# A retention and MLP kernel: eight load requests for the first weight matrix are renumbered

## The chip, the cores and the metric

The kernel runs on one core of a Trainium2 chip. The metric is the device time of one execution in microseconds. A core has five engines that run side by side, each through its own instructions in order: PE (matrix products, with its weight loads listed as PEld), DVE (elementwise work), ACT (activation functions and copies), POOL (elementwise work, and the requests for some transfers) and SP (the requests for the other transfers). They wait for each other by semaphores. Transfers between the main memory and the core's own memory are done by 16 DMA engines that all the requests share.

## The reference

For 8 batches, 8 heads, 576 positions and a head size of 64, a retention layer is computed: scores of q and k, times a decay that falls with the distance and is zero ahead of the position, times v. Its result x, one row of 512 numbers for each of the 4608 tokens, goes through a two-layer MLP with a tanh GELU between.

```python
scores = scale * np.matmul(q, k.transpose(0, 1, 3, 2))
Dmat = np.where(rel >= 0, gamma[:, None, None] ** rel[None, :, :], 0.0)
ret = scores * Dmat[None, :, :, :]
attn_out = np.matmul(ret, v)
x = attn_out.transpose(0, 2, 1, 3).reshape(B * S, H * D)      # 4608 x 512
h = x @ w_in                                                  # 512 x 2048
g = 0.5 * h * (1.0 + np.tanh(c * (h + 0.044715 * h * h * h)))
out = g @ w_out                                               # 2048 x 512
```

## The kernel before, in words

**Tiling.** A batch is cut into five units of positions: four of 128 and a tail of 64. The units are numbered through, so 40 in all. The MLP works on nine blocks of 512 tokens. Matrix products take fp16 and add up in fp32 in PSUM banks.

**The order is written out by hand.** `ORDER` (lines 17 to 123) is a list of steps, and the loop at line 1044 issues them one after the other. Each engine gets its instructions in the order of this list. A step is a letter with numbers, and `do` (line 1030) tells which function it calls. The steps that matter here:

| step | function, line | what it does |
|---|---|---|
| `I,g,g` | `load_w_in`, 248, through `load_w`, 236 | POOL requests piece g of w_in, cast to fp16 on the way (line 238) |
| `J,g,g` | `load_w_out`, 258 | POOL requests piece g of w_out |
| `L,u,n` | `load`, 208 | SP requests q, k or v of unit u |
| `N,t,fc,part` | `mm1`, 750 | PE: 256 hidden columns (fc and fc+1, of 128 each) for half a token block: 8 matrix products at line 757 |
| `F,t,fc,part` | `gelu`, 764 | ACT: GELU of what `N` computed |
| `Y`, `X`, `R` | 624, 609, 653 | PE: scores, state products and output of a pair of wide units (lines 636, 619, 665 and 677) |
| `t`, `y` | `pe_T`, 489, `copy_T`, 498 | PE transposes (line 493), and the copy of what they gave |
| `a`, `m`, `z` | 703, 684, 724 | sums of the state (DVE, line 713), masking (DVE, line 644), cast of the state (POOL) |
| `K,n` | `busy`, 999 | n matrix products on an identity that nobody reads (line 1003) |
| `O,t,u` | `mm2`, 777 | PE: a quarter of the second layer's sum for 128 tokens, line 783 |

**The pieces of w_in.** w_in is 512 x 2048. Piece g is a block of 256 rows and 512 columns, by `f, c = divmod(g, 2)`: f is the block of columns (hidden blocks 4f to 4f+3) and c is the half of the rows. So pieces 0 and 1 are the two halves of f=0, 2 and 3 of f=1, 4 and 5 of f=2, 6 and 7 of f=3. All eight are of one size, 256 KB as they land.

**How mm1 reads them.** One `N` step computes its two blocks of 128 hidden columns one after the other, and each is four products over the four quarters of the 512 rows: quarters 0 and 1 lie in the even piece, 2 and 3 in the odd piece. So the first two of its 8 products need the even piece alone, and the third needs the odd one.

```python
for i in range(TB // n):
    for ct in range(NCT):
        nc.tensor.matmul(
            hps[:, i, :],
            w_in_sb[:, ct, 128 * (fc + i) : 128 * (fc + i) + 128],
```

**The order of PE's steps around the change** (lines 21 to 23 of the list, PE's steps alone): `R,0`, `Y,2,1`, `K,3`, `N,0,2,0`, `N,0,0,0`, `N,0,12,0`, `Y,2,0`, `N,0,4,0`, `X,2`, `t,4,k`, `t,4,q`, `N,0,8,0`, `N,0,10,0`, `R,2`. By the hidden columns, these first readers are of f=0 (`N,0,2` and `N,0,0`), f=3 (`N,0,12`), f=1 (`N,0,4`) and f=2 (`N,0,8`), in that order.

**The order on POOL.** The eight `I` steps stand at eight places among POOL's other work: the first behind the setup, the second behind the decay rows, then three in a row, a cast of k, and three in a row again. In this document the places are called s1 to s8.

Of the kernel before, what the change touches and what calls it, by code (L numbers as in the profile page):

```python
# [14 lines left out]
I32 = mybir.dt.int32  # L15

ORDER = """
L,0,1 b Z,1,v L,0,0 L,0,2 L,2,1 L,2,0 I,2,g q,0 k,0,g Z,2,g g,g I,7,g K,4 K,4 K,4 K,3 K,4 t,0,q,h
L,2,2 L,4,1 c t,0,k,h I,1,g v,0,v X,0 y,0,k,v I,0,g I,3,g a,0,1 y,0,q,v Z,3,v k,2,g K,4 K,4 Y,0,1
t,2,k,o m,0,1 z,0,1,a I,6,g K,4 Y,0,0 a,1,1 q,2 L,4,0 K,4 t,2,q,h m,0,0 y,2,k,a y,2,q,v I,4,g K,1  # L20
R,0 I,5,g x,0 Y,2,1 L,5,0 x,1 i,4,v K,3 N,0,2,0 N,0,0,0 o,1,1 m,2,1 L,5,1 Z,4,g v,2,v F,0,2,0
N,0,12,0 Y,2,0 F,0,0,0 z,1,1,v N,0,4,0 L,5,2 X,2 k,4,g Z,5,v q,4 F,0,12,0 F,0,4,0 t,4,k,o a,2,1
t,4,q,o a,3,1 y,4,q,a N,0,8,0 L,4,2 z,2,1,g L,9,1 N,0,10,0 F,0,8,0 k,5,g m,2,0 L,7,1 R,2 F,0,10,0
y,4,k,v B,4,-1 q,5 x,3 x,2 N,0,14,0 L,7,0 t,5,q,o N,0,0,1 L,7,2 J,1,g F,0,14,0 N,0,6,0 y,5,q,v J,3,g
# [1051 lines left out]
```

## Time and profile before

| what | value |
|---|---|
| time, median of 3 runs (lowest to highest) | 297.25 us (296.75 to 297.45) |
| time of the profiled execution | 296.55 us |
| its span in the profile | 294.8 us |
| PE busy | 281.6 us, 96% of the span |
| DVE, ACT, POOL busy | 73%, 51%, 38% |
| transfers | 36.70 MB read, 9.44 MB written |
| requests for w_in | 8 on POOL, median 9.1 us from request to landing |

The profile has one line for each group of like instructions: its line of code, engine, operation, the tile that it writes `<-` the tiles that it reads, count, time busy and mean, and the idle time of the engine ahead of it with what ended that. The timeline lists instructions in order of time: start, duration, engine, line, tiles, count, and in brackets the idle time before. The chain that ended last goes back from the last instruction through whatever released each step. A busy PE is not a PE at its peak, since matrix products overlap: a product of 128x256 is listed with 273 ns, but in a row they start about 109 ns apart.

### The profile page before, as it was taken

The page shows a single profiled execution, that of the slowest core. Times are in us where ns is not written, and L with a number is a line of the kernel's source. Part 1 is how long each engine was busy: PE and PEld are TensorE (multiplying, and loading weights), DVE is VectorE, ACT ScalarE, POOL GpSimd, SP SyncE. Part 2 cuts the span into 40 slices and gives each one's busy share as a digit, 9 for nine tenths or more (in the row PEclk, how much of TensorE's full clock was granted, in tenths as well). Part 3 has the DMA queues.
Part 4 walks back from the last instruction along what each step waited for, and adds up shares of the span by engine and source line. Part 5 has one row for each costly group of instructions (what it writes and reads, how often), then busy time and mean ns, then how long its engine had stood idle before and what let it go on. Part 6 is the DMA issues. An engine that isn't in the chain of part 4 may idle for free.

```text
span 294.8 us, 9645 instructions
## 1 busy us (share of the span) xinstructions
PE 281.6 (96%) x4067; PEld 235.7 (80%) x4067; DVE 214.7 (73%) x437; ACT 149.9 (51%) x288; POOL 111.8 (38%) x178
## 2 busy tenths in 40 slices
PE   7686999999999999999999999999999999999995
PEld 2354986667888888888888888888888888888873
DVE  7694763686865779576678699599889988977740
ACT  2143674334634553554554646546777587665411
POOL 7941920404361084163415644783466223000000
PEclk9999999999999999999999999999999999999999
DMA  6999999995989999999099997899488570002112
GB/s 192 284 252 242 221 219 211 217 205 129 244 119 247 167 190 213 207 248 216 17 239 197 183 196 169 202 189 161 130 194 197 75 216 6 37 26 83 73 42 103
DMA packets 136428, 49.79 MB, mean 169 GB/s; under 512 B 118208, under 2 KB 130880, under 8 KB 136384
## 3 DMA queue, kind: packets, MB, share of 16 engines
q1 hardware_dynamic: 132032, 44.97, 75.5%
q0 software_dynamic: 4352, 4.20, 8.6%
q8 instruction: 32, 0.52, 0.8%
q14 instruction: 12, 0.10, 0.1%
HBM read 36.70 MB, written 9.44 MB: 156 GB/s over the span
## 4 chain that ended last, share of the span: by engine, by line
PE 84%; DMA 6%; POOL 5%; DVE 2%; issue 1%; ACT 1%; ACTq 0%; POOLq 0%
PE bank L860 30%; PE bank L757 27%; PE bank L957 12%; PE bank L783 6%; DMA w_in_sb<-in_moe_w_in_dram 4%; PE x L529 2%; PE sk L553 2%; DMA pages<-in_k_dram 2%; POOL w_in_sb L238 1%; PE sk L563 1%; PE x L574 1%; DVE pages L817 1%; POOL wide L269 1%; DMA out_dram<-ost 1%; PE bank L493 1%
## 5 line engine op out<-in xcount | busy, mean ns | idle before, releaser
L757 PE MATMUL bank<-xT,w_in_sb 128*128 128x256 f16 x768 | 94.4, 273 | 2.9 <-DMA w_in_sb<-in_moe_w_in_dram 2.9
L765 ACT ACTIVATE gT<-bank 128x512 f16<-128x512 f32 x96 | 56.7, 598 | 62.4 <-PE bank L757 60.5
L757 PEld LDWEIGHTS <-w_in_sb 128*128 128x128 f16 x768 | 73.7, 98 | 14.5 <-DMA w_in_sb<-in_moe_w_in_dram 3.7
L860 PEld LDWEIGHTS <-ssum 128*128 128x128 f16 x480 | 46.3, 98 | 6.4 <-issue 0.8
L269 POOL CAST sz<-s 64x256 f16<-64x256 f32 x48 | 24.5, 510 | 66.1 <-DVE s L713 44.8
L860 PE MATMUL bank<-tsum,ssum 128*128 128x256 f16 x360 | 46.0, 273 | 0.6 <-DVE ost L817 0.6
L860 PEld LDWEIGHTS <-gT 128*128 128x128 f16 x360 | 34.7, 98 | 4.4 <-issue 0.2
L424 POOL TENSOR_TENSOR qk<-pages,dec 128x512 f16<-128x512 f32 (+1 forms) x20 | 21.5, 1087 | 32.5 <-PE x L619 12.5
L860 PE MATMUL bank<-w_out_sb,gT 128*128 128x256 f16 x240 | 31.1, 273 | 0.0
L424 POOL TENSOR_TENSOR v<-pages,dec 128x512 f16<-128x512 f32 (+1 forms) x20 | 21.5, 1074 | 14.2 <-DMA pages<-in_v_dram 11.4
L817 DVE TENSOR_TENSOR ssum<-gT 128x1024 f16<-128x1024 f16 x30 | 23.5, 784 | 4.1 <-ACT gT L765 3.7
L817 DVE TENSOR_TENSOR ost<-u,bank 128x256 f32<-128x256 f32 x45 | 18.1, 415 | 9.4 <-PE bank L860 9.1
L817 DVE TENSOR_TENSOR ssum<-gT,ssum 128x1024 f16<-128x1024 f16 x30 | 23.4, 781 | 0.2
L691 DVE TENSOR_TENSOR ret<-sk,mask 128x512 f16<-128x512 f32 (+1 forms) x32 | 19.8, 617 | 4.7 <-PE sk L563 4.4
L957 PEld LDWEIGHTS <-pages 128*128 128x128 f16 x192 | 18.4, 98 | 2.8 <-issue 0.3
L957 PE MATMUL bank<-pages 128*128 128x256 f16 x144 | 20.3, 273 | 0.3 <-ACT pages L267 0.3
L783 PE MATMUL bank<-w_out_sb,gT 128*128 128x512 f16 x80 | 19.1, 380 | 0.0
L817 DVE TENSOR_TENSOR u<-u,bank 128x256 f32<-128x256 f32 x30 | 12.4, 415 | 8.8 <-PE bank L860 5.9
L593 ACT ACTIVATE xT<-x 128x512 f16<-128x512 f32 (+1 forms) x25 | 14.3, 578 | 7.9 <-PE x L574 7.9
L713 DVE TENSOR_TENSOR s<-s,sk 128x256 f32<-128x256 f32 x36 | 14.9, 414 | 4.6 <-PE sk L563 4.0
L817 DVE TENSOR_TENSOR hc<-hc,bank 128x512 f32<-128x512 f32 x21 | 14.4, 684 | 4.8 <-PE bank L957 2.3
L267 ACT COPY hc<-bank 128x512 f32<-128x512 f32 x19 | 11.1, 585 | 12.5 <-PE bank L957 12.5
(114 smaller groups left out, 428.3 us busy)
## 6 DMA issues: line engine op xcount, KB each, us to landing
out_dram<-ost SPq DMA_DIRECT2D x35, 256.0 KB, 3.4
pages<-in_q_dram SPq DMA_DIRECT2D x32, 256.0 KB, 4.7
pages<-in_v_dram SPq DMA_DIRECT2D x24, 256.0 KB, 4.0
pages<-in_k_dram SPq DMA_DIRECT2D x24, 256.0 KB, 4.3
pages<-in_k_dram SPq DMA_DIRECT2D x4, 512.0 KB, 7.0
pages<-in_v_dram SPq DMA_DIRECT2D x4, 512.0 KB, 6.6
w_in_sb<-in_moe_w_in_dram POOLq DMA_DIRECT2D x8, 256.0 KB, 9.1
w_out_sb<-in_moe_w_out_dram POOLq DMA_DIRECT2D x8, 256.0 KB, 10.5
```

Of the source, the lines that this page charges most:

```text
L267: nc.scalar.copy(out=o, in_=i)
L269: (nc.vector if eng == "v" else nc.gpsimd).tensor_copy(out=o, in_=i)
L424: eng.tensor_tensor(out=out, in0=s["raw"][:, i, 0:n], in1=dec[:, i // 2, s["j"], 0:n].unsqueeze(2).to_broadcast([128, n, D]), op=ALU.mult,)
L593: nc.scalar.activation(out=xT[:, :, o : o + G * (b - a)].rearrange("c p (h s) -> c p h s", s=G), in_=x[:, a:b].rearrange("c h p s -> c p h ...
L691: nc.vector.tensor_tensor(out=ret[:, :, 0:n], in0=now["two"][:, :, 0, 0:n], in1=mask.unsqueeze(1).unsqueeze(1).to_broadcast([128, 2, n, G] ...
L713: nc.vector.tensor_tensor(out=s32, in0=state[0], in1=kv, op=ALU.add)
L757: nc.tensor.matmul(hps[:, i, :], w_in_sb[:, ct, 128 * (fc + i) : 128 * (fc + i) + 128], xT[:, ct, TB * t % XR + lo : TB * t % XR + hi], st ...
L765: nc.scalar.activation(out=gTs[t][:, fc : fc + TB // (hi - lo), lo:hi], in_=h.pop((t, fc, lo)), func=AF.Gelu_apprx_tanh, bias=0.0, scale=1.0,)
L783: nc.tensor.matmul(ops[t, tcc], gTs[t][:, ft, 128 * tcc : 128 * tcc + 128], w_out_sb[:, ft, :], start=(ft == 0), stop=(ft == NFC - 1),)
L817: (nc.vector if eng == "v" else nc.gpsimd).tensor_tensor(out=out, in0=a, in1=b, op=op)
L860: nc.tensor.matmul(p["ps", bank][:, HN * col : HN * col + HN], a[:, k], b[:, k], start=(k == 0 and i in (1, 6)), stop=(k == HK - 1), skip_ ...
L957: nc.tensor.matmul(p["ps", bank][:, n], w[:, c, 128 * n : 128 * n + 128], x[:, c], start=(n == 0 and c == 0 and i in (1, 2, 5)), stop=(c = ...
```

## The change

The eight requests keep their places in the list. What changes is which piece is asked for at which place:

| place | s1 | s2 | s3 | s4 | s5 | s6 | s7 | s8 |
|---|---|---|---|---|---|---|---|---|
| piece before | 2 | 7 | 1 | 0 | 3 | 6 | 4 | 5 |
| piece after | 1 | 0 | 6 | 2 | 4 | 5 | 7 | 3 |

```diff
-L,0,1 b Z,1,v L,0,0 L,0,2 L,2,1 L,2,0 I,2,g q,0 k,0,g Z,2,g g,g I,7,g K,4 K,4 K,4 K,3 K,4 t,0,q,h
-L,2,2 L,4,1 c t,0,k,h I,1,g v,0,v X,0 y,0,k,v I,0,g I,3,g a,0,1 y,0,q,v Z,3,v k,2,g K,4 K,4 Y,0,1
-t,2,k,o m,0,1 z,0,1,a I,6,g K,4 Y,0,0 a,1,1 q,2 L,4,0 K,4 t,2,q,h m,0,0 y,2,k,a y,2,q,v I,4,g K,1
-R,0 I,5,g x,0 Y,2,1 L,5,0 x,1 i,4,v K,3 N,0,2,0 N,0,0,0 o,1,1 m,2,1 L,5,1 Z,4,g v,2,v F,0,2,0
+L,0,1 b Z,1,v L,0,0 L,0,2 L,2,1 L,2,0 I,1,g q,0 k,0,g Z,2,g g,g I,0,g K,4 K,4 K,4 K,3 K,4 t,0,q,h
+L,2,2 L,4,1 c t,0,k,h I,6,g v,0,v X,0 y,0,k,v I,2,g I,4,g a,0,1 y,0,q,v Z,3,v k,2,g K,4 K,4 Y,0,1
+t,2,k,o m,0,1 z,0,1,a I,5,g K,4 Y,0,0 a,1,1 q,2 L,4,0 K,4 t,2,q,h m,0,0 y,2,k,a y,2,q,v I,7,g K,1
+R,0 I,3,g x,0 Y,2,1 L,5,0 x,1 i,4,v K,3 N,0,2,0 N,0,0,0 o,1,1 m,2,1 L,5,1 Z,4,g v,2,v F,0,2,0
```

## The prediction

> **What bounds the kernel now.** I read the page first. Its chain that ended last lies mostly on PE, with a share for DMA:
>
> ```profile
> PE 84%; DMA 6%; POOL 5%; DVE 2%; issue 1%; ACT 1%; ACTq 0%; POOLq 0%
> ```
>
> Next I asked for the busy time by stretch. Columns: stretch, its length, then PE, PEld, DVE, ACT and POOL busy with their counts, PE's granted clock, DMA share, GB/s.
>
> ```profile
> 20.00:30.00 10.00, 7.00 (x113) 5.01 (x113) 5.68 (x11) 4.82 (x8) 1.35 (x4) 1.00 1.15 243
> 30.00:40.00 10.00, 10.00 (x184) 8.87 (x182) 7.68 (x12) 6.77 (x12) 8.56 (x13) 1.00 1.07 221
> 40.00:50.00 10.00, 10.00 (x152) 7.72 (x150) 4.74 (x5) 6.46 (x11) 0.00 (x0) 1.00 1.22 216
> ```
>
> PE has holes before 30 us and none behind. The change lies in the first stretch. The chain in order of time (start, length, what) tells which wait ends last there:
>
> ```profile
> 15.33 1.38 POOL w_in_sb L238 x2
> 16.71 12.46 DMA w_in_sb<-in_moe_w_in_dram
> 29.17 0.05 issue
> 29.21 1.70 PE bank L757 x14
> 30.92 0.45 PE x L665 x8
> ```
>
> It is the eighth request for w_in: asked for at 16.71, landed at 29.17, and from there PE never stops. So the time hangs on how much PE work is left when the last piece lands. PE's timeline shows it step by step:
>
> ```profile
> 20.46 0.82 PE L1003 MATMUL bank<-ident 128*128 128x512 f16 x3
> 21.12 1.91 PE L757 MATMUL bank<-xT,w_in_sb 128*128 128x256 f16 x16
> 25.35 1.05 PE L757 MATMUL bank<-xT,w_in_sb 128*128 128x256 f16 x8 [2.31 <-DMA w_in_sb<-in_moe_w_in_dram]
> 26.32 0.42 PE L636 MATMUL sk<-qkT 64*64 64x128 f16 x16
> 26.67 1.05 PE L757 MATMUL bank<-xT,w_in_sb 128*128 128x256 f16 x8
> 27.65 0.45 PE L619 MATMUL x<-wide,wide 64*64 64x64 f16 x32
> 28.03 0.40 PE L493 MATMUL bank<-ident,qk 128*128 128x128 f16 x4
> 28.26 0.38 PE L757 MATMUL bank<-xT,w_in_sb 128*128 128x256 f16 x2
> 29.21 1.70 PE L757 MATMUL bank<-xT,w_in_sb 128*128 128x256 f16 x14 [0.57 <-DMA w_in_sb<-in_moe_w_in_dram]
> 30.75 0.44 PE L665 MATMUL x<-qkT,sz 128*128 128x128 f16 x5
> ```
>
> By lines and counts these are K,3; N,0,2 and N,0,0; N,0,12; Y,2,0; N,0,4; X,2; t,4; two products of N,0,8; its other six with N,0,10; R,2. N,0,8 ran its two products on piece 4 and stopped at the third, which needs piece 5: so the wait is for the half that a product reads, not for the whole group. The table has each place's landing: the request's start in POOL's timeline plus its time to landing, asked for one by one.
>
> | | s1 | s2 | s3 | s4 | s5 | s6 | s7 | s8 |
> |---|---|---|---|---|---|---|---|---|
> | asked | 4.01 | 8.27 | 12.10 | 12.82 | 13.53 | 15.28 | 16.00 | 16.71 |
> | to landing | 8.2 | 7.4 | 7.6 | 8.2 | 10.0 | 10.0 | 11.2 | 12.5 |
> | landed | 12.2 | 15.7 | 19.7 | 21.0 | 23.5 | 25.3 | 27.2 | 29.2 |
>
> The answers for s6, s7 and s8:
>
> ```profile
> DMA to landing us min/median/max: 10.0/10.0/10.0
> ...
> DMA to landing us min/median/max: 11.2/11.2/11.2
> ...
> DMA to landing us min/median/max: 12.5/12.5/12.5
> ```
>
> The 25.35 wait ends with s6 (25.3) and the 29.21 wait with s8 (29.2), so these landings are what PE sees.
>
> **The change part by part.** Nothing is added or removed. The requests keep their places on POOL, and nothing on POOL or SP up to 17 us waits for w_in, so I leave the eight landings where they are and move only the readers.
>
> *Pieces 1 and 0 go from s3, s4 to s1, s2* (landed 15.7 instead of 21.0). N,0,2 gains nothing that counts: K,3's three products of some 0.21 us from 20.46 hold PE to 21.1 anyway, it started at 21.12, and a hole of over 2 us follows. Cost: 0.
>
> *Piece 6 goes to s3 and piece 7 from s2 to s7.* N,0,12 reads both. Its first two products can go at 22.9, when N,0,0 is done; the third waits for 27.2. Six are left: eight products ahead of a step of small ones took 26.67 to 27.65 = 0.98, two of them at 0.109 (1.75 for 16 in the chain) are 0.22, so six are 0.76. N,0,12 ends at 28.0 instead of 26.3, Y,2,0 (26.32 to 26.67, 0.35) at 28.35.
>
> *Piece 3 goes from s5 to s8, 4 and 5 from s7, s8 to s5, s6, and 2 from s1 to s4.* The first unready reader behind Y,2,0 is now N,0,4: two products on piece 2 end at 28.6, the third waits for piece 3 at 29.2. This wait takes the place of N,0,8's. Behind 29.21 PE then has six of N,0,4 (0.76), X,2 (27.65 to 28.03, 0.38), t,4 (0.23), N,0,8 and N,0,10 (16 at 0.109, 1.75): 3.12 us, so R,2 starts at 32.33. Before it was 30.75, so **+1.58 us**. The delay at N,0,12 costs nothing of its own, as 28.6 is 0.6 ahead of 29.2; without that cover each microsecond would cost one.
>
> *Who is queued behind.* X,2 is 2.32 later (29.97 against 27.65), more than R,2 is. On DVE the state sums of line 713 move from 28.16 to 30.5 and the mask of line 644 from 29.02 to 31.3, ending at 32.6. R,2's second part, which reads it, began 0.54 behind its first (31.29), so now at 32.87: 0.3 to spare. The copy for B,4 and the scaling of q for t,5 (30.36, 1.33 long) end at 34.0; t,5 moves from 32.81 to 34.4: fits. POOL waited 8.52 us for the first state sum and cast from 28.64; that and the eight w_out requests behind it (30.55 to 37.85) come 2.3 later. Asked singly, the third, fourth, sixth and eighth of them landed after 9.5, 10.7, 11.3 and 13.3 us, at 41.5, 43.4, 46.9 and 50.4. The first reader of w_out is at 44.91, those of the second to fourth quarters at 47.52, 51.69 and 54.30, and all of them move by 1.6: at least 2.6 are left. Landings could differ among the SP loads that they now meet; by bounds, 0 to about 1 us of it reaching PE. I take 0, nearest to those gaps. ACT has 0.98 of idle in one piece at 38 and follows PE.
>
> *Whether it reaches the end.* PE is full from 29.2, so a delay is handed on unless a later wait eats it. All that PE's waits behind 31 us offer is this:
>
> ```profile
> PE bank L860 <- DVE ost L817: 0.6, 1, 0.6
> PE bank L957 <- DVE pages L817: 0.4, 1, 0.4
> PE bank L957 <- ACT pages L267: 0.3, 1, 0.3
> ```
>
> None ends in a transfer. They lie at 220 to 230 us, and the chain enters them from PE (219.95), so DVE's and ACT's work there shifts along. Bounds: 0 to 1.3 eaten; I take 0.
>
> *Sum.* The profiled execution took 296.55 (span 294.8 and 1.75 around it): 296.55 + 1.58 = 298.13. That execution lies 0.70 below the median of the runs, 297.25, and the result is a median, so I put the same step on it: **298.8 us**, +0.5%. Telling this kernel from no change takes about 0.2%, 0.6 us: its three runs spread over 0.70.
>
> *The longer hole in PE.* Before, the longest was 2.31 us, and the products behind it ran at full pace. Now only two products lie between 23.3 and 27.2, a hole of 3.9 us, which this trace doesn't have. What it has is PE's start: the 19 products of 128x512 from 1.96 on begin 0.43 apart up to 6.63 and 0.21 apart behind it, though the granted clock stands at 1.00 in every stretch. So PE can run at half pace after idleness. Bounds: 0 (as after 2.31 us) to a slow stretch of 4.7 us like the one at the start. I take 0: 3.9 is nearer to 2.31 than to a PE that had never worked. [...]
>
> **The rivals.**
>
> *PE drops to half pace in the hole.* Place: 23.3 to 27.2; it decides if the hole is long enough. Slow for 4.7 us from 27.25: six products 1.4, Y,2,0 0.7, two products 0.45 (29.8, s8 is in), six 1.4, X,2 0.7, which is 31.9; t,4 and 16 products 1.98 at full pace: R,2 at 33.9, 3.15 later than before: 300.4. For: the slow start. Against: full pace after 2.31 us.
>
> *The delay is eaten.* If all 1.3 of PE's later waits go, 297.5. Against: the chain runs through PE into them.
>
> *Faster: the late places land sooner.* s7 and s8 took 11.2 and 12.5, while s2 took 7.4 for the same bytes. Landing after L, R,2 would start at 16.04 + L + 0.76 + 0.35 + 0.98 + 0.38 + 0.23 + 1.75 = 20.5 + L, as s7 then binds. It decides below L = 9.6; at 9.0 R,2 starts at 29.5, and the time is 296.0. For: equal pieces differ by 5 us. Against: the DMA share is at 1.12 to 1.23 throughout 12 to 29 us, and neither sizes, places nor the SP loads change.
>
> *It doesn't do what it says.* The order of first readers is f=0, f=3, f=1, f=2, and in that order the requests would be 1, 0, 6, 7, 2, 3, 4, 5. Piece 7 stands seventh and 3 last. With the literal order N,0,8 would again wait for s8 with the same 14 products behind: 297.25, no change. The diff is what runs, so this is no case of its own, but the reason for the sign.
>
> **How the numbers follow.** N,0,4 waiting for the last piece: 0.73, alone 298.2 to 299.4 (landing of s8 against s7, half a microsecond, and the runs' spread). Half pace: 0.12, 299.8 to 300.6. Eaten: 0.10, 297.2 to 297.8. Faster: 0.05. The first case holds the likeliest time, 298.8. The range from 297.9 to 300.3 leaves out eaten, faster and some of half pace, 0.2 in all. Slower by over 0.2%: the first two, 0.85, less a little for the spread and more for the top of the third: 0.85. Within: 0.10. Faster: 0.05.
>
> **What would show it.** In PE's timeline: N,0,2 still near 21.1; two products of line 757 near 22.9, a wait for w_in ending near 27.2, six products and Y,2,0; two products, a short wait ending near 29.2; then six products, X,2, t,4 and 16 products without a hole, and R,2's line 665 near 32.3. Half pace would show as products of 128x256 starting 0.21 apart behind 27.2. The w_out requests start near 32.9, and no wait for w_out appears at line 783. Wrong would be: another place binding, s7 or s8 landing over 1 us off, a new PE wait for DVE at R,2 or t,5, or waits at 220 to 230 us that shrink by the delay.

## The result, and the profile after

The changed kernel takes 299.57 us (median of 9 runs, 298.48 to 301.04), beside it the kernel before 297.45 (9 runs, 296.75 to 298.76). The ratio is 1.0072, with a 95% interval of 1.0046 to 1.0098: slower by 2.1 us, inside the range, and 0.8 us above the predicted 298.8. The profiled execution took 298.48 us with a span of 296.7. Later the same kernel was timed twice more, each time beside the kernel before: 1.0129 (1.0106 to 1.0153) and 1.0089 (1.0057 to 1.0121).

The page's chain by engine has hardly moved:

```profile
PE 85%; DMA 5%; POOL 4%; DVE 2%; issue 1%; ACT 0%; ACTq 0%; POOLq 0%
```

The chain in order of time (start, length, what) shows another request than before:

```profile
15.33 11.01 DMA w_in_sb<-in_moe_w_in_dram
...
26.38 1.46 PE bank L757 x6
27.84 0.57 PE sk L636 x16
28.41 1.47 PE bank L757 x8
```

It is the seventh request, piece 7, that PE waits for last; behind it PE runs without a stop. PE's timeline of the same stretch:

```profile
21.62 2.13 PE L757 MATMUL bank<-xT,w_in_sb 128*128 128x256 f16 x18
26.38 1.46 PE L757 MATMUL bank<-xT,w_in_sb 128*128 128x256 f16 x6 [2.63 <-DMA w_in_sb<-in_moe_w_in_dram]
27.77 0.64 PE L636 MATMUL sk<-qkT 64*64 64x128 f16 x16
28.35 1.53 PE L757 MATMUL bank<-xT,w_in_sb 128*128 128x256 f16 x8
29.81 0.44 PE L619 MATMUL x<-wide,wide 64*64 64x64 f16 x32
...
30.42 1.91 PE L757 MATMUL bank<-xT,w_in_sb 128*128 128x256 f16 x16
32.17 0.61 PE L665 MATMUL x<-qkT,sz 128*128 128x128 f16 x8
```

The first line holds 18 products: N,0,2, N,0,0 and the first two of N,0,12, as foreseen. Then the hole, the other six, Y,2,0, N,0,4, X,2, t,4, N,0,8 with N,0,10, and R,2 at 32.17, 1.42 us later than before. But six products took 1.39 us from start to the next step's start, and Y,2,0 took 0.58 instead of 0.35. The busy times by stretch say why; the first figure behind the five engines' is PE's granted clock:

```profile
24.00:26.00 2.00, 0.00 (x0) 0.00 (x0) 0.70 (x2) 0.17 (x1) 0.00 (x0) 0.99 1.19 219
26.00:28.00 2.00, 1.62 (x18) 0.96 (x22) 0.00 (x0) 0.12 (x1) 0.00 (x0) 0.50 1.16 261
28.00:29.00 1.00, 1.00 (x20) 0.65 (x13) 0.00 (x0) 0.48 (x1) 0.00 (x0) 0.50 1.13 327
29.00:30.00 1.00, 1.00 (x29) 0.66 (x31) 0.00 (x0) 0.08 (x1) 0.00 (x0) 0.81 0.93 188
```

The clock is at 0.50 from about 25.96 (0.99 over two microseconds is 0.04 us at half) to 29.38 (0.81 over one is 0.38). So the rival "PE drops to half pace in the hole" is there, together with the forecast order of work. In this one execution two things soften it. POOL was 0.67 us ahead of the profile of before, 0.56 of it since a select at line 397 took 0.85 instead of 1.41 us for its pair. Piece 7 landed at 26.3 and piece 3 at 28.3, both 0.9 us ahead of the forecast. And PE, at half pace, came to N,0,4's third product only after piece 3 had landed: the forecast second wait is gone, its place taken by slow work. So it is luck that R,2 came within 0.2 us of the forecast 32.33: from a landing at 28.3 the forecast 3.12 us of work would have brought it to 31.4, and half pace took back most of what the early landing gave.

To follow the delay to the end I compared the starts of 24 marks of PE (the products of line 553) with those of the profile of before. It is 1.42 us at the first, at 69.58 us in the profile before, 1.51 at 191.33 and 1.80 at 241.25. Nothing ate it.

### The profile page after: what moved, and what is told of

Same layout as the page of the kernel before. It is cut to its first block, busy times and chain, and to the rows that moved or that the text cites. A ratio compares the mean times of both kernels' runs of the same rounds, so it can differ in the third digit from the quotient of the medians.

```text
span 296.7 us, 9645 instructions
## 1 busy us (share of the span) xinstructions
PE 284.0 (96%) x4067; PEld 236.6 (80%) x4067; DVE 214.7 (72%) x437; ACT 149.9 (51%) x288; POOL 113.6 (38%) x178
## 4 chain that ended last, share of the span: by engine, by line
PE 85%; DMA 5%; POOL 4%; DVE 2%; issue 1%; ACT 0%; ACTq 0%; POOLq 0%
PE bank L860 30%; PE bank L757 28%; PE bank L957 12%; PE bank L783 6%; DMA w_in_sb<-in_moe_w_in_dram 4%; PE x L529 2%; PE sk L553 2%; DMA pages<-in_k_dram 1%; PE sk L563 1%; PE x L574 1%; PE bank L987 1%; POOL w_in_sb L238 1%; DVE pages L817 1%; PE bank L493 1%; POOL wide L269 1%
## 5 line engine op out<-in xcount | busy, mean ns | idle before, releaser
L757 PE MATMUL bank<-xT,w_in_sb 128*128 128x256 f16 x768 | 95.4, 275 | 2.6 <-DMA w_in_sb<-in_moe_w_in_dram 2.6
L269 POOL CAST sz<-s 64x256 f16<-64x256 f32 x48 | 26.2, 545 | 66.7 <-DVE s L713 46.2
L424 POOL TENSOR_TENSOR qk<-pages,dec 128x512 f16<-128x512 f32 (+1 forms) x20 | 20.8, 1047 | 29.9 <-DMA pages<-in_q_dram 12.0
L424 POOL TENSOR_TENSOR v<-pages,dec 128x512 f16<-128x512 f32 (+1 forms) x20 | 22.2, 1112 | 15.4 <-DMA pages<-in_v_dram 10.9
L817 DVE TENSOR_TENSOR ssum<-gT 128x1024 f16<-128x1024 f16 x30 | 22.9, 764 | 3.5 <-ACT gT L765 3.1
L817 DVE TENSOR_TENSOR u<-u,bank 128x256 f32<-128x256 f32 x30 | 12.5, 415 | 9.1 <-PE bank L860 6.1
L644 DVE TENSOR_TENSOR ret_wide<-sk,maskw 128x1024 f16<-128x1024 f32 x8 | 9.8, 1221 | 11.0 <-PE sk L636 11.0
```

What stands on the lines that cost most here:

```text
L269: (nc.vector if eng == "v" else nc.gpsimd).tensor_copy(out=o, in_=i)
L424: eng.tensor_tensor(out=out, in0=s["raw"][:, i, 0:n], in1=dec[:, i // 2, s["j"], 0:n].unsqueeze(2).to_broadcast([128, n, D]), op=ALU.mult,)
L644: nc.vector.tensor_tensor(out=wide_ret()[:, 2 * part : 2 * part + 2].rearrange("c p l j s -> c p l (j s)"), in0=sk.rearrange("c l p j s -> ...
L757: nc.tensor.matmul(hps[:, i, :], w_in_sb[:, ct, 128 * (fc + i) : 128 * (fc + i) + 128], xT[:, ct, TB * t % XR + lo : TB * t % XR + hi], st ...
L817: (nc.vector if eng == "v" else nc.gpsimd).tensor_tensor(out=out, in0=a, in1=b, op=op)
```

## The experiments

All orders are of the eight pieces at the places s1 to s8; the change is 1, 0, 6, 2, 4, 5, 7, 3. Each comparison is with runs of the kernel before on the same chip. "Delay" is the lag of the first mark, 69.58 us in the profile before.

### The order of the readers, in earnest

```diff
- 1, 0, 6, 2, 4, 5, 7, 3
+ 1, 0, 6, 7, 2, 3, 4, 5
```

> Requests in the order 1, 0, 6, 7, 2, 3, 4, 5, which is the order of the first readers by both halves. Theory A (the time follows the PE work that is left when the last piece lands): the last piece is read by N,0,8 again with 14 products left, so as the kernel before, 297.4 us, ratio 1.000; in the timeline N,0,12 runs through from 22.9 and the last wait for w_in ends near 29.2 in the third product of N,0,8. Rival B (asking for f=0 first is itself what costs, by landings that move): as the changed kernel, 299.6.

Ratio 1.0015 (0.9987 to 1.0042), 296.96 against 296.86 us. N,0,12 ran through, 24 products in a row from 20.82. Its last wait ended at 29.57 in N,0,8's third product, with 14 products behind it; the last request went out at 16.4 and took 13.1 us. Asking for f=0 first costs nothing, and the words of the change, taken literally, give no gain either. One stretch of 3.41 us at half pace takes 0.006 off an execution's mean granted clock. Four of the twelve have a mean of 0.983 to 0.989, so two such stretches or more, and three of these four are the slowest (299.12 to 300.42 us): slow stretches are not confined to the change.

### The first part alone

```diff
- 2, 7, 1, 0, 3, 6, 4, 5     (before)
+ 1, 0, 2, 7, 3, 6, 4, 5
```

> Only the first part of the change: 1, 0, 2, 7, 3, 6, 4, 5, so pieces 1 and 0 are asked for first and 2 and 7 take the third and fourth place, while the last four places are as before. Theory A: N,0,2 starts where K,3 lets it, the waits for s6 and s8 stay with the same work behind them: ratio 1.000. Rival (the early pieces of f=0 let PE start sooner and shorten the first stretch): 0.998 or lower.

1.0004 (0.9983 to 1.0024). The waits ended at 25.91 and 29.68, with 14 products behind the second. The part costed at nothing is worth nothing that can be told from noise.

### Piece 7 moved to the last place

```diff
- 1, 0, 6, 2, 4, 5, 7, 3
+ 1, 0, 6, 2, 4, 5, 3, 7
```

> The changed kernel with pieces 7 and 3 exchanged: 1, 0, 6, 2, 4, 5, 3, 7. The last piece is now read by N,0,12. Theory A: behind its landing at 29.2 stand six products of N,0,12 (0.76), Y,2,0 (0.35), N,0,4 (0.98), X,2 (0.38), t,4 (0.23), N,0,8 and N,0,10 (1.75), 4.45 us against 1.54 before: +2.9 for the order, and a hole of 6 us that drops PE to half pace for some 3.4 us, up to 1.7 more: 300.4 to 302.0. Rival B (what counts is only that f=0 came first, or that the pieces land in another order): 299.6.

1.0171 (1.0143 to 1.0199), 301.65 us, as expected. The hole is 6.11 us, the clock stands at 0.50 from 24.74 to 34.98, and the delay in the profile, the slowest of the six executions (302.79 us), is 5.25 us. PE resumed at 28.80, so the 4.45 us of work would have ended at 33.25; R,2 started at 36.00, and the 2.75 between are the slow stretch. The loss grew with the work behind the last piece and with the time at half pace; no run has this order at full pace, so the order's own part is by the sum.

### Pieces 3 and 5 exchanged

```diff
- 1, 0, 6, 2, 4, 5, 7, 3
+ 1, 0, 6, 2, 4, 3, 7, 5
```

> The changed kernel with pieces 3 and 5 exchanged: 1, 0, 6, 2, 4, 3, 7, 5. The last piece is read by N,0,8 as before, but piece 7 is still asked for seventh. Theory A: N,0,12's third product waits for s7 (27.2) and 4.45 us of PE work stand behind it without another wait, so R,2 starts at 31.7 against 30.75: +0.95, ratio 1.003, and up to 1.006 with the drop to half pace in the hole that remains. Rival E (only the reader of the last piece counts, and the seventh is covered): as before, ratio 1.000.

1.0085 (1.0058 to 1.0113). The rival that only the last piece's reader counts is out. The profiled execution behaves as by theory A, with one wait, for s7, and none behind it; but piece 7 landed at 26.6 and the clock held at 1.00 behind the hole of 2.20 us, so its delay is only 0.31, and it ran 298.35 us where the median was 299.26. The median is more than the order's 0.95 us explains. Half pace in the other executions would fit. Their traces are not there, but their mean granted clocks are: three of the other five, at 0.983 to 0.989, had at least two slow stretches. Where these lay is open.

### Pieces 5 and 7 exchanged: two short holes for one long

```diff
- 1, 0, 6, 2, 4, 5, 7, 3
+ 1, 0, 6, 2, 4, 7, 5, 3
```

> The changed kernel with pieces 5 and 7 exchanged: 1, 0, 6, 2, 4, 7, 5, 3. The last piece is still read by N,0,4, but N,0,12 waits only for s6, so PE's long hole is cut from about 4 us (products' starts) to about 2.4. Theory A with a drop to half pace in the long hole: the order's 1.58 us stays and the drop goes: 299.0 us, granted clock above that of the changed kernel. Rival C (the drop costs nothing, the order is all): as the changed kernel, 299.6. Rival D (the position of piece 7 is all): as before, 297.4.

1.0097 (1.0061 to 1.0134), 299.91 us instead of the 299.0 of theory A. Rival C's 299.6 is nearer, but not for its reason, since the profile has a slow stretch. Both holes were short, 2.29 and 2.32 us, and the clock fell at 27.27, between two stretches of work, and stayed at 0.50 up to 34.10; the delay is 3.75 us. So a hole of 2.3 us can be enough, and my condition, one long hole, is wrong.

### Busy products in the hole

```diff
-N,0,12,0 Y,2,0 F,0,0,0 z,1,1,v N,0,4,0 ...
+F,0,0,0 K,7 K,7 N,0,12,0 Y,2,0 z,1,1,v N,0,4,0 ...
```

> The changed kernel with two steps K,7 (14 products on the identity, 3.0 us, that nobody reads) ahead of N,0,12, inside the hole in which PE waits for piece 7; nothing else of the work differs. Theory A with the drop: PE stays at full pace behind 26 us, 298.8 to 299.0, the granted clock near 0.997 and the spread of the runs smaller. Rival C (no cost of the drop): 299.6 or, where the extra products hold up N,0,12, up to 0.3 more.

1.0059 (1.0036 to 1.0082), 298.51 us. The GELU step `F,0,0,0` stands ahead of the products here; the order of ACT's own steps stays the same. PE's timeline of this run is the forecast one, wait by wait:

```profile
22.20 3.18 PE L1003 MATMUL bank<-ident 128*128 128x512 f16 x14
25.22 0.38 PE L757 MATMUL bank<-xT,w_in_sb 128*128 128x256 f16 x2
27.27 0.83 PE L757 MATMUL bank<-xT,w_in_sb 128*128 128x256 f16 x6 [1.67 <-DMA w_in_sb<-in_moe_w_in_dram]
28.03 0.42 PE L636 MATMUL sk<-qkT 64*64 64x128 f16 x16
28.38 0.39 PE L757 MATMUL bank<-xT,w_in_sb 128*128 128x256 f16 x2
29.26 0.83 PE L757 MATMUL bank<-xT,w_in_sb 128*128 128x256 f16 x6 [0.49 <-DMA w_in_sb<-in_moe_w_in_dram]
...
32.38 0.61 PE L665 MATMUL x<-qkT,sz 128*128 128x128 f16 x8
```

The waits end at 27.27 and 29.26 (forecast 27.2 and 29.2), R,2 starts at 32.38 (32.33), the clock is 1.00 throughout, and the delay is 1.63. This is the order's price by itself. The expected smaller spread is not there: its eleven runs lie from 296.81 to 299.70. On that chip the changed kernel was not timed, so the two were run side by side:

> The changed kernel once more, only so that the run with busy products in its hole stands beside it on one chip. Expected 1.007 to 1.013, as the two comparisons so far have it, with a drop to half pace behind the hole in the profile.

> The changed kernel with 14 busy products in its hole, beside the changed kernel itself. Theory A with the drop (order 1.58 us, the rest of the changed kernel's loss is half pace): ratio 1.005 to 1.006, and 0.5 to 2 us below the changed kernel on this chip. Rival C (half pace costs nothing): the two are equal within 0.3 us.

The changed kernel: 1.0089 (1.0057 to 1.0121), 300.01 us. With busy products: 1.0034 (1.0018 to 1.0049), 298.13 us. The intervals don't overlap: adding 14 useless products to PE makes the changed kernel 1.9 us faster by the medians, 1.6 by the ratios. The gain is in the expected 0.5 to 2 us, the ratio itself below the expected 1.005. In the profile with them the delay is 1.68, but it is not the forecast wait: PE was late there (N,0,2 at 23.01) and the useless products held it up to 27.78, while the last two pieces landed at 25.5 and 27.2, so PE never waited for w_in. The profile without has a drop that comes late:

```profile
26.96 0.83 PE L757 MATMUL bank<-xT,w_in_sb 128*128 128x256 f16 x6 [2.94 <-DMA w_in_sb<-in_moe_w_in_dram]
27.72 0.42 PE L636 MATMUL sk<-qkT 64*64 64x128 f16 x16
28.07 0.39 PE L757 MATMUL bank<-xT,w_in_sb 128*128 128x256 f16 x2
28.92 1.46 PE L757 MATMUL bank<-xT,w_in_sb 128*128 128x256 f16 x6 [0.46 <-DMA w_in_sb<-in_moe_w_in_dram]
```

PE came out of its hole at full pace: six products in 0.76. Only then, at about 28.7, the clock fell, and the next six took 1.39. These two stretches of the same run hold the fall (0.84 over one microsecond is 0.32 us at half):

```profile
28.00:29.00 1.00, 0.54 (x15) 0.19 (x4) 0.00 (x0) 0.43 (x1) 0.00 (x0) 0.84 1.16 316
29.00:31.00 2.00, 2.00 (x40) 1.28 (x41) 0.00 (x0) 0.58 (x1) 0.00 (x0) 0.50 0.88 182
```

### The changed kernel on another chip

> The changed kernel itself, for a comparison on the chip of the three other runs beside it. Expected again 0.7% above the kernel before, some 299 us where that takes 296.9, with the runs spread over more than 2 us and the granted clock between 0.983 and 0.995, because the windows in which PE drops to half pace fall differently in each run.

1.0129 (1.0106 to 1.0153), 300.17 us, above what I expected. The profiled execution is the slowest of its five (301.42 us): a hole of 3.28 us, the clock at 0.50 from 26.35 to 33.18, and a delay of 3.55 us.

### Busy products in the hole of the kernel before

```diff
-N,0,12,0 Y,2,0 F,0,0,0 z,1,1,v N,0,4,0 ...
+F,0,0,0 K,5 K,5 N,0,12,0 Y,2,0 z,1,1,v N,0,4,0 ...
```

> The kernel before with two steps K,5 (10 products on the identity, 2.15 us) in its own hole of 2.31 us ahead of N,0,12. If that hole also drops PE to half pace in some executions, 0.1 to 0.3% faster than the kernel before; if a hole of 2.31 us is short enough, or what is lost there is covered by the wait for the last piece, 1.000.

0.9991 (0.9968 to 1.0015). The kernel before loses nothing measurable in its own hole, so the loss by half pace belongs to the change, not to both kernels alike.

### A version that uses the cover

With the literal order, N,0,14 and N,0,6 are moved ahead of the wait for the last piece:

```diff
-N,0,12,0 Y,2,0 F,0,0,0 z,1,1,v N,0,4,0 L,5,2 X,2 k,4,g Z,5,v q,4 F,0,12,0 F,0,4,0 t,4,k,o a,2,1
+N,0,12,0 F,0,0,0 N,0,14,0 Y,2,0 z,1,1,v F,0,12,0 N,0,4,0 F,0,14,0 N,0,6,0 L,5,2 X,2 k,4,g Z,5,v q,4 F,0,4,0 F,0,6,0 t,4,k,o a,2,1
...
-y,4,k,v B,4,-1 q,5 x,3 x,2 N,0,14,0 L,7,0 t,5,q,o N,0,0,1 L,7,2 J,1,g F,0,14,0 N,0,6,0 y,5,q,v J,3,g
+y,4,k,v B,4,-1 q,5 x,3 x,2 L,7,0 t,5,q,o N,0,0,1 L,7,2 J,1,g y,5,q,v J,3,g
...
-... v,5,v J,2,g L,9,2 F,0,6,0 N,0,8,1 ...
+... v,5,v J,2,g L,9,2 N,0,8,1 ...
```

> Requests in the literal order 1, 0, 6, 7, 2, 3, 4, 5, and two steps of mm1 whose pieces have landed are moved ahead of the last wait: N,0,14 behind N,0,12 and N,0,6 behind N,0,4 (with their GELUs). Theory A: 16 products of 0.109, 1.75 us, leave the work behind the last landing and fill holes: 1.6 to 1.8 us faster than the kernel before, ratio 0.994. Rival F (the wait moves on: GELUs on ACT, or DVE's sums behind X,2, hold PE at R,2): between 0.997 and 1.000.

0.9981 (0.9961 to 1.0001): a third of what was expected, and not clear of no change. It lies where rival F has it, and PE does wait for DVE instead: 0.48 us ahead of 31.99, behind R,2 (DVE's line 439). In its profile PE no longer waits for w_in at all and is 1.50 us ahead at the first mark, near the 1.6 to 1.8 expected; at the last it is 0.42 ahead. With the wait gone, PE's own late start counts: N,0,2 started at 22.12, not 21.12 (more on this below). And of the 1.08 us lost between the first mark and the last, 0.85 go between the marks at 194.61 and 207.68, where PE waits for DVE (line 817) twice, 0.9 us in all behind 190 us; the profile of before has 0.4 in one wait. But 0.58 of it is a jump that most other profiles have too (below), so it can't all be charged to this version. How the rest of the expected gain went stays open.

Then the constants that POOL makes late go behind the last request as well:

```diff
-L,2,2 L,4,1 c t,0,k,h I,6,g ...
+L,2,2 L,4,1 t,0,k,h I,6,g ...
...
-R,0 I,5,g x,0 ...
+R,0 I,5,g c x,0 ...
```

> As the run with the two steps moved ahead, and besides POOL makes its late constants (3.06 us from 9.04 to 12.10 in the profile before) behind the last request for w_in, so that six requests go out 2 to 3 us earlier. Theory G (a landing is set by the request's time): the last piece lands some 2 us earlier, ratio 0.988 to 0.990. Rival H (a landing is set by what the 16 DMA engines, at 1.12 to 1.23 of their share, can move by then): times to landing grow by as much as the requests move up, ratio 0.994 as without it.

0.9964 (0.9948 to 0.9980), 295.76 us: the only version whose interval lies below the kernel before. It is above both forecasts, and against the version without this step (0.9961 to 1.0001) the gain is not clear of noise. The requests of s6 to s8 start at 12.7, 13.4 and 14.1 instead of 15.3, 16.0 and 16.7, and take 10.3, 11.3 and 12.4 us, as long as before. So the last piece lands at 26.5, 2.7 us sooner: theory G is right on the landing, and wrong on the time, since PE had no wait for w_in left to shorten:

```profile
20.52 3.66 PE L757 MATMUL bank<-xT,w_in_sb 128*128 128x256 f16 x32
24.10 0.42 PE L636 MATMUL sk<-qkT 64*64 64x128 f16 x16
24.45 1.92 PE L757 MATMUL bank<-xT,w_in_sb 128*128 128x256 f16 x16
```

PE goes through N,0,12, N,0,14, N,0,4 and N,0,6 without a hole; behind them it waits for DVE instead, 0.50 us ahead of 27.46 (line 424) and 0.21 ahead of 30.78 (line 439). It is 2.2 us ahead from the first mark to 194.61 and 1.04 at the last.

## Why the prediction was right, and where it was not

**What bounds the kernel: right.** The time hangs on the PE work left behind the last pieces' landings. Four orders bear it out: the same work behind (the literal order, the first part alone) gives 1.0015 and 1.0004, more work gives 1.0072 to 1.0129 for the change and 1.0171 for piece 7 in the last place. The last two include half pace as well as work.

**Pieces 1 and 0 first: cost 0, right** (1.0004, with an interval of 0.2% to either side).

**N,0,4 waits for the last piece, +1.58 us: right, seen alone in one profile.** In the first run with busy products the clock held, both waits came as forecast, and the delay is 1.63. That N,0,12's later end costs nothing of its own holds in that timeline, where N,0,4 still waited 0.49 for piece 3. The 1.68 of the second such run came by another way, without a wait. The times of the two are 1.0059 and 1.0034, which is 1.8 and 1.0 us; the interval of the second, 0.5 to 1.5 us, lies just below 1.58. Of the three profiles of the changed kernel itself only one has the wait for piece 3 (0.46 us, up to 28.92); in the other two PE at half pace came after the landing.

**Those queued behind: right.** R,2 followed N,0,10 directly in every profile of the changed kernel, and none shows a wait for DVE or for w_out there, although POOL's w_out requests began at 32.71 instead of 30.55.

**It reaches the end: right.** 1.42 us at the first mark, 1.80 at the last. The other two profiles of the changed kernel also end with more delay than they began with (2.68 to 3.70 and 3.55 to 4.98), so here no later wait ate it. In the two runs with busy products the delay ended at 2.1 and 1.4 us, having stood at 2.25 and 2.27 at 221 us: so a part can be eaten there.

**The longer hole, "I take 0": wrong, and it is the step that failed.** I gave half pace 0.12, an estimate, and it is in all three profiles of the changed kernel, from 25.96, 26.35 and 28.68 on. The other executions bear it out by their mean granted clocks: none of the 20 of the changed kernel is above 0.994, so each had at least one slow stretch, while 33 of the 74 of the kernel before beside the experiments and 8 of the 23 with busy products are at 0.997 or more. Two stretches or more (0.989 or less) are in 11 of the 20, against 9 of the 74 and 1 of the 23. A mean doesn't tell where a stretch lay.

I reasoned that a hole of 3.9 us was nearer to one of 2.31, behind which PE kept its pace. The length of one hole does not sort these runs. Two holes of 2.3 us with 1.5 us of work between them also ended at half pace, and in the run with the hole of 2.94 us the clock fell 1.7 us after the hole was over. What the traces have in common is this. In each profile that shows them the changes of the clock lie whole multiples of 3.41 us apart (in the first one of the changed kernel at 12.31, 15.72, 25.96 and 29.38), so its time can be cut into windows of 3.41 us that begin or end at these changes (in the profile before, at its one fall, at 293.78). For each window at full clock behind the first 8 us or so I take PE's busy share, as the profile has it. In the 13 windows that were followed by a fall within the first 40 us the share was 29 to 44%. Every window up to 290 us that no fall followed, in the eleven profiles whose mean granted clock is below 1.000, had 46% or more. The other three (the literal order, the first run with busy products, the version with the constants moved) are at 1.000 and had next to nothing at half pace. The first line is the window of the changed kernel ahead of its fall at 25.96 (1.20 of 3.41 us, 35%), the second one of the kernel before, whose hole lies in two windows with 2.31 and 2.19 us of work (68 and 64%):

```profile
22.55:25.96 3.41, 1.20 (x11) 0.82 (x9) 2.07 (x5) 1.20 (x3) 0.00 (x0) 1.00 1.19 219
...
24.13:27.54 3.41, 2.19 (x32) 1.65 (x32) 0.14 (x1) 0.60 (x1) 0.00 (x0) 1.00 1.18 231
```

The edges of the windows lie elsewhere from profile to profile (25.96, 26.35 and 25.26 near the hole in the three of the changed kernel), so the hole was cut otherwise in each. In the 3.4 us ahead of 25.35 the kernel before has only 1.09 us of work, a third; its windows were cut otherwise, and its clock held. This is what these eleven profiles have in common; no run varies the share to find the limit.

The price is what the side-by-side runs have between them, 0.55% or 1.6 us (1.9 by the medians). The rival's own sum has 3.15 for the order and half pace together, so 1.57 for half pace: its price was right, and its chance was not. The slow stretches at the holes last 3.41 us (twice), 6.83 (twice) and 10.24: one, two and three times 3.41.

**The number.** 298.8 was 297.25 and 1.58. The first comparison has 2.12 us between the medians, 0.54 more than that; the two later ones have 3.25 (300.17 against 296.92) and 2.81 (300.01 against 297.2), 1.7 and 1.2 more. Where the busy products ran beside it, they took away 1.88 of the 2.81: the missing term is half pace. That is more than the 1.2 missing there, so beside those runs the order by itself was worth 0.9 us and not 1.58. The range held with some luck: 299.57 lies between the 298.2 to 299.4 of the first case and the 299.8 to 300.6 of the rival, and a step of 3.25, as in the second comparison, would have been 300.5, above the range.

**It doesn't do what it says: right.** The literal order is 1.0015, and the placed one slower.

## What to carry to other kernels

Cost a new order of requests by the work that stands behind the last landing, not by how early the first piece comes: the order of the first readers gained nothing here by itself (1.0015). Where a wait of a few microseconds opens in TensorE's work, count its busy share over some 3.4 us around the wait: here the clock fell behind windows of 3.41 us with 29 to 44% of work and held behind those with 46% or more, and two holes of 2.29 and 2.32 us cost as much (1.0097) as one long one (1.0072 to 1.0129). Products that nobody reads, put into the hole, were worth 1.9 us here. And a wait that is filled up with work can move the bound to what it used to hide (here PE then waited for DVE, 0.48 us in one version and 0.50 and 0.21 in the other), so look there before counting the whole gain.

## What the runs showed that I had not expected

- **PE works at half pace ahead of the first stretch in many executions.** In eight of the 13 profiles taken with and after the result, the granted clock was at 0.50 for some 3.4 us that began between 11.6 and 13.7, behind PE's holes around 10 to 12.7, and N,0,2 started between 21.62 and 23.01. In the other five and in the profile before it started between 20.42 and 21.12. With the last four places as before it isn't felt: in the run of the first part alone N,0,2 started at 22.24, PE still had to wait for both pieces, and the time is 1.0004.
- **Requests made earlier landed earlier.** With the constants moved the last three requests went out 2.6 us earlier and took 10.3, 11.3 and 12.4 us, against 10.0, 11.2 and 12.5. The times to landing are not fixed, though: over the 14 profiles the last request took 11.5 to 13.1 us.
- **A part of the spread lies far from the change.** Between the marks at 201.15 and 207.68 the delay jumps by 0.57 to 0.59 us in ten of the 13 profiles, by 0.3 in one and not at all in two, the changed kernel's first among them. With the last four places as before it is there in one (pieces 1 and 0 first) and missing in another (busy products in the hole of the kernel before). In exactly these ten, POOL's product for v (line 424) came late, behind a wait of 1.0 to 1.5 us, and ran into one of DVE's products (line 721 or 424), which then took 1.26 us; in the other four profiles, that of before included, the two don't overlap and DVE's products took 0.41. PE then waited for what DVE had next (0.51 us ahead of 202.90 in the run of the first part alone).
